# Gate rows as one-column products sent through DRAM, the inverse table moved ahead in the queue, LN2 columns among the first inverse tiles, table scaling on GpSimd

## The chip, the cores and the metric

One core of one Trainium2 chip. The metric is the device time of one execution in microseconds (us). PE is TensorE, DVE is VectorE, ACT is ScalarE, POOL is GpSimd and SP is SyncE, which issues most transfers. PSUM is the memory that PE writes; all other tiles named here lie in SBUF. Timelines are in us from the start of the profiled execution.

## The reference

```python
mod = (silu(c) @ w_mod).reshape(1, 6, 1, 640)
sa, ca, ga, sb, cb, gb = mod[:, 0], ..., mod[:, 5]
h = layernorm(x) * (1 + ca) + sa
x = x + ga * irfft2(rfft2(h) * (w_r + 1j * w_i))          # x: 2048 x 640, bf16
h = layernorm(x) * (1 + cb) + sb
x = x + gb * ((silu(h @ w_gate) * (h @ w_up)) @ w_down)    # 640 -> 1728 -> 640
```

The kernel does the transforms as matmuls with tables. Three stages matter here: the filter (products with the complex filter, in 21 groups of columns), the inverse transform (16 tiles of 128 rows), and the second half, LN2 and the gate and up products. `ga` and `gb` are needed as rows repeated over 128 partitions, `sb` and `cb` (the "LN2 columns") as columns.

## The kernel before

The gate rows come from matmuls whose stationary operand is the gate vector repeated 128 times, so that every partition receives the row:

```python
def mod_bc(j, lo, bank, o=0, ks=range(NC5)):            # 5 matmuls of 320 columns
    gps_ = psum[:, bank, o:o + 320]
    for k in ks:
        nc.tensor.matmul(gps_, lhsT=sc_rep[:, k, :], rhs=wm_r[:, k, j, lo:lo + 320], ...)
```

The queue of SP between the filter's own loads and the weights of the second half:

```python
nc.sync.dma_start(wm_r[:, :, 0, :], wm_m[:, :, 0, :])   # ga weights, before the filter halves
# ... filter halves, tables ...
t2_dma(0); t2_dma(1); t2_dma(2); t2_dma(3)              # transposes of the forward transform
nc.sync.dma_start(wm_r[:, :, 1:3, :], wm_m[:, :, 1:3, :])  # LN2 weights, 1600 KB
nc.sync.dma_start(wm_r[:, :, 3, :], wm_m[:, :, 3, :])      # gb weights, 800 KB
nc.sync.dma_start(Htab[:], H_dram)
nc.sync.dma_start(RI[:], RI_dram)                       # inverse table, 320 KB
```

The seam between filter and inverse transform (the two halves of the table RI are multiplied by `ga` on DVE):

```python
    if g == NG - 1:
        rot(40, 8, slice(0, 64), nc.vector, (1,))       # a rotation: scaled copy, 128 x 512
        nc.vector.tensor_tensor(RI[:, 1], RI[:, 1], ga_bc[:], ALU.mult)
nc.scalar.copy(gb_bc[:, 320:640], mod_bc(3, 320, 3, 128))
s1em(0)                                                 # first inverse tile
s1em(1)
for q0, q1 in ((0, 8), (8, 32), (32, 64)):
    rot(64, 16, slice(q0, q1), nc.vector)
nc.vector.tensor_tensor(RI[:, 0], RI[:, 0], ga_bc[:], ALU.mult)
```

In the inverse loop, at tile 4, the first chunk of LN2 is transposed by DMA (tile `h2T`), and at tile 10 POOL scales it (four of its five parts; ACT the fifth); the first gate product of PE reads it, just before the products of the last tile:

```python
    if t == 4:
        ln2_tr(0)                                       # transpose by DMA: h2T
        load_gu(512, 1024, (1,))
    if t in (10, 13):
        ln2_mod(0, range(4) if t == 10 else range(4, 5))   # scaling on POOL, then the fifth on ACT
    if t == NT - 1:
        fin13 = gu13(0, at_of(0))                       # first gate product
```

## Time and profile before

| | before |
|---|---|
| median of 3 runs | 250.89 us (250.81 to 251.66) |
| span of the profiled run, mean clock | 249.1 us, 0.998 |
| PE busy | 98% |
| first product from a transposed column group starts on PE | 42.60 us |
| last filter product of DVE ends | 60.26 us |
| first inverse product (L1149) | 64.75 us |
| h2T: transpose issued, POOL scales from | 71.83, 77.80 us |
| first gate product, then the run of gate products | 81.28, 82.38 us |

The prediction below shows the lines for most of this. First the chain of work that ended last, as shares of the span by engine:

```profile
PE 80%; SPq 9%; DMA 6%; ACT 1%; DVE 1%; issue 1%; DVEq 0%; ACTq 0%
```

Then, from DVE's timeline (start, duration, line, operation, output<-input), one of the last rotations, 0.28 us for 512 columns, and the multiplication of one half of RI by `ga`:

```profile
62.39 0.28 DVE L646 TENSOR_SCALAR rE<-rE 128x512 bf16<-128x512 bf16 x1
62.59 0.48 DVE L711 TENSOR_TENSOR rH<-rH,ga_bc 128x640 bf16<-128x640 bf16 x1
```

### The profile page before, as it was taken

The page shows a single profiled execution, that of the slowest core. Times are in us where ns is not written, and L with a number is a line of the kernel's source. Part 1 is how long each engine was busy: PE and PEld are TensorE (multiplying, and loading weights), DVE is VectorE, ACT ScalarE, POOL GpSimd, SP SyncE. Part 2 cuts the span into 40 slices and gives each one's busy share as a digit, 9 for nine tenths or more (in the row PEclk, how much of TensorE's full clock was granted, in tenths as well). Part 3 has the DMA queues.
Part 4 walks back from the last instruction along what each step waited for, and adds up shares of the span by engine and source line. Part 5 has one row for each costly group of instructions (what it writes and reads, how often), then busy time and mean ns, then how long its engine had stood idle before and what let it go on. Part 6 is the DMA issues. An engine that isn't in the chain of part 4 may idle for free.

```text
span 249.1 us, 6473 instructions
## 1 busy us (share of the span) xinstructions
PE 243.5 (98%) x2512; PEld 200.4 (80%) x2512; DVE 209.7 (84%) x524; ACT 162.7 (65%) x300; POOL 74.3 (30%) x122
## 2 busy tenths in 40 slices
PE   8999999999999999999999999999999999999994
PEld 3778877999889888688877778886768887779973
DVE  4798888998898997879997997879995888895895
ACT  3778666997788798488862487674356766235740
POOL 8487755894025422000003900001330000440000
PEclk9999999999999999999999999999999999999999
DMA  7999999999999999300005020003311000211001
GB/s 221 396 357 334 309 365 191 175 397 381 286 352 288 275 264 186 81 9 0 3 0 108 13 68 29 3 3 58 73 42 39 3 0 3 54 53 57 3 0 53
DMA packets 45760, 34.43 MB, mean 138 GB/s; under 512 B 21731, under 2 KB 42658, under 8 KB 45346
## 3 DMA queue, kind: packets, MB, share of 16 engines
q1 hardware_dynamic: 43936, 30.00, 42.8%
q0 software_dynamic: 1504, 3.95, 6.7%
q8 instruction: 19, 0.31, 0.5%
q10 hardware_dynamic: 290, 0.08, 0.1%
q14 instruction: 11, 0.09, 0.1%
HBM read 26.72 MB, written 4.72 MB: 126 GB/s over the span
## 4 chain that ended last, share of the span: by engine, by line
PE 80%; SPq 9%; DMA 6%; ACT 1%; DVE 1%; issue 1%; DVEq 0%; ACTq 0%
PE psum L1016 33%; PE psum L899 19%; PE psum L986 9%; DMA rW<-wflip_r 4%; PE psum L879 3%; PE psum L597 3%; PE psum L664 3%; PE psum L567 2%; SPq L273 2%; SPq L277 2%; PE psum L1149 2%; DMA rM<-in_w_mod_dram 2%; SPq L275 2%; PE psum L1152 2%; PE psum L974 2%; PE psum L618 2%
## 5 line engine op out<-in xcount | busy, mean ns | idle before, releaser
L1016 PEld LDWEIGHTS <-rW 128*128 128x128 bf16 (+1 forms) x528 | 46.9, 98 | 5.6 <-issue 0.2
L1016 PE MATMUL psum<-rW 128*128 128x256 bf16 (+1 forms) x240 | 27.1, 259 | 0.0
L913 POOL TENSOR_TENSOR rM<-rM,rL 128x320 f32<-128x320 f32 x6 | 5.9, 975 | 68.2 <-ACT rL L912 68.2
L899 PEld LDWEIGHTS <-rE 128*128 128x128 f16 (+1 forms) x196 | 19.1, 97 | 7.7
L1016 PE MATMUL psum<-rY,rW 128*128 128x256 bf16 (+1 forms) x96 | 24.0, 259 | 0.0
L986 PE MATMUL psum<-rW 128*128 128x256 bf16 (+1 forms) x170 | 23.1, 291 | 0.0
L899 PE MATMUL psum<-rE 128*128 128x320 f16 (+1 forms) x147 | 22.3, 299 | 0.0
L590 DVE TENSOR_TENSOR rM<-psum,rW 128x384 bf16<-128x384 f32 (+2 forms) x42 | 20.1, 541 | 2.0 <-PE psum L567 1.4
L986 PEld LDWEIGHTS <-rW 128*128 128x128 bf16 x170 | 16.6, 98 | 3.8
L1016 PEld LDWEIGHTS <-rE 128*128 128x128 f16 x192 | 17.4, 98 | 2.4
L899 PEld LDWEIGHTS <-rX 128*128 128x128 bf16 (+1 forms) x151 | 14.6, 97 | 5.4
L760 POOL TENSOR_TENSOR rstd<-rstd,mhalf 128x4 f32<-128x4 f32 (+2 forms) x4 | 4.5, 1120 | 48.2 <-DVE rstd L756 48.2
L1052 DVE TENSOR_TENSOR rH<-psum,rW 128x512 bf16<-128x512 f32 x21 | 14.5, 689 | 4.9 <-PE psum L1016 3.1
L1048 ACT COPY rH<-psum 128x512 f32<-128x512 f32 x21 | 12.3, 585 | 9.0 <-PE psum L1016 7.3
L1042 ACT COPY rW<-psum 128x512 f32<-128x512 f32 x21 | 12.3, 585 | 6.8 <-PE psum L1016 6.7
L1055 ACT COPY rX<-psum 128x512 f32<-128x512 f32 x21 | 12.3, 586 | 6.7 <-PE psum L1016 6.7
L1070 DVE TENSOR_TENSOR rX<-rH,rL 128x512 bf16<-128x512 bf16 x21 | 8.9, 423 | 9.1 <-ACT rL L1068 9.0
L382 DVE SCALAR_TENSOR_TENSOR rE<-rE,mv,psum 128x648 bf16<-128x648 f32 (+1 forms) x17 | 14.2, 844 | 2.1 <-PE psum L318 1.5
L1056 DVE TENSOR_TENSOR rX<-psum,rX 128x512 f32<-128x512 f32 x21 | 14.4, 685 | 1.7 <-ACT rX L1055 1.6
L899 PE MATMUL psum<-rA,rX 128*128 128x320 bf16 (+1 forms) x98 | 15.6, 299 | 0.0
L1016 PE MATMUL psum<-rH,rW 128*128 128x256 f16 (+1 forms) x96 | 15.1, 259 | 0.1
L1016 PE MATMUL psum<-rE,rY 128*128 128x256 f16 (+1 forms) x96 | 15.1, 259 | 0.0
(198 smaller groups left out, 674.3 us busy)
## 6 DMA issues: line engine op xcount, KB each, us to landing
out_dram<-rA SPq DMA_DIRECT2D x31, 80.0 KB, 1.6
rM<-in_w_mod_dram SPq DMA_DIRECT2D x3, 800.0 KB, 9.9
rX<-in_A_x_dram SPq DMA_DIRECT2D x3, 640.0 KB, 7.3
rA<-in_B_w_down_dram SPq DMA_DIRECT2D x2, 960.0 KB, 14.4
rM<-in_w_mod_dram SPq DMA_DIRECT2D x1, 1600.0 KB, 7.1
rY<-in_B_w_gate_dram POOLq DMA_DIRECT2D x2, 768.0 KB, 7.7
rW<-in_B_w_gate_dram SPq DMA_DIRECT2D x2, 640.0 KB, 7.2
rW<-in_B_w_up_dram SPq DMA_DIRECT2D x2, 640.0 KB, 6.5
```

The lines of the kernel that those rows point to most:

```text
L382: nc.vector.scalar_tensor_tensor(Zv[:, h], Cv[:, h], mv[:, t, 0:1], zps[:, h], ALU.mult, ALU.subtract)
L590: nc.vector.tensor_tensor(PP[:, :, hl], xv[:, :, hl], in1, ALU.mult)
L597: nc.tensor.matmul(yps[:, i, :], lhsT=_rev(PP, 64 * n * ps + i, [[n, 128]]), rhs=identb[:], start=(ps == 1 and i == 0), stop=(ps == 0 and ...
L899: nc.tensor.matmul(o, lhsT=lhsT, rhs=rhs, start=start, stop=stop, skip_group_check=True)
L986: nc.tensor.matmul(gu[u], lhsT=Wgu[:, u, c5, ff * 128:(ff + 1) * 128], rhs=h2T[:, :, c5, :], start=(c5 == 0), stop=(c5 == NC5 - 1))
L1016: nc.tensor.matmul(o[:, f], lhsT=w, rhs=b, start=(start and f == 0 and i == 0), stop=(stop and f == F - 1 and i == len(ops) - 1), skip_gro ...
L1042: nc.scalar.copy(c0, X)
L1048: nc.scalar.copy(c2, X)
L1052: nc.vector.tensor_tensor(c11, Z, c0, ALU.add)
L1055: nc.scalar.copy(c3, X)
L1056: nc.vector.tensor_tensor(c22, Y, c3, ALU.add)
L1070: nc.vector.tensor_tensor(ato, v4(c11), v4(g21), ALU.mult)
```

## The change

Its intent is to take work off PE and DVE. The 20 matmuls of 320 columns give way to 50 one-column products, which make the gate as five columns; those are transposed by a small matmul, written to DRAM as one row and read back into all 128 partitions. The ga weights move behind the filter halves, so the filter lands earlier; RI moves ahead of the transposes; the LN2 weights go to the end of this stretch of the queue; the LN2 columns are made between the first inverse tiles, instead of in the filter's last groups; and POOL, not DVE, multiplies RI by `ga`. The core of the diff (cuts marked):

```diff
-    nc.sync.dma_start(wm_r[:, :, 0, :], wm_m[:, :, 0, :])
...
         nc.sync.dma_start(Ktab[:, 0:384], K_dram[:, 0:384])
+        nc.sync.dma_start(wm_ga[:], wm_m[:, :, 0, :])
+        nc.sync.dma_start(RI[:], RI_dram)
...
-        t2_dma(3)
-        nc.sync.dma_start(wm_r[:, :, 1:3, :], wm_m[:, :, 1:3, :])
-        nc.sync.dma_start(wm_r[:, :, 3, :], wm_m[:, :, 3, :])
-        nc.sync.dma_start(Htab[:], H_dram)
-        nc.sync.dma_start(RI[:], RI_dram)
+        def g_row(i, eng, row):
+            eng.dma_start(row[:], bass.AP(tensor=g_dram[i].tensor, offset=g_dram[i].offset, ap=[[0, P], [1, D]]))
+        def mod_col(o, w, c5):                       # five one-column products
+            for k in range(NC5):
+                nc.tensor.matmul(o, lhsT=w[:, k, 128 * c5:128 * c5 + 128], rhs=sc_col[:, k:k + 1], ...)
...                                                  # in stage_a
+            if g == 7:
+                nc.sync.dma_start(wm_r[:, :, 2, :], wm_m[:, :, 3, :])      # gb weights
+                g_write(0, nc.sync)
+                t2_dma(3)
+                g_row(0, nc.sync, ga_bc)
+                nc.sync.dma_start(Htab[:], H_dram)
+                nc.sync.dma_start(wm_r[:, :, 0:2, :], wm_m[:, :, 1:3, :])  # LN2 weights
...
+        wsum(Wn, 0, 16, nc.vector)                   # filter sums, cut smaller
...
+            if g == 4:
+                wsum(Wn, 16, 32, nc.vector)
...
+            if g == NG - 5:
+                g_write(1, nc.gpsimd)
+                ri_fold(1)                           # RI[:, 1] times ga, on POOL
...
+                rot(40, 8, slice(0, 64), nc.vector)  # both rotations of the last group, on DVE
-                rot(40, 8, slice(0, 64), nc.vector, (1,))
-                nc.vector.tensor_tensor(RI[:, 1], RI[:, 1], ga_bc[:], ALU.mult)
...
-        nc.scalar.copy(gb_bc[:, 320:640], mod_bc(3, 320, 3, 128))
-        s1em(0)
-        s1em(1)
+        ri_fold(0)
+        for t in range(2):
+            s1em(t)
+            if t == 0:
+                b_cols(0)                            # LN2 columns
+        g_row(1, nc.gpsimd, gb_bc)
...
-        nc.vector.tensor_tensor(RI[:, 0], RI[:, 0], ga_bc[:], ALU.mult)
+        VTs = {0: s1er(0)}
+        b_cols(1)
+        VTs[1] = s1er(1)                             # and tiles are then prepared two ahead
```

## The prediction

> **What bounds the kernel now.** I read the page's busy shares first, then the chain of work that ended last in order of time, then the timelines of the DMA-issuing queue, VectorE (DVE), TensorE (PE) and GpSimd (POOL) around the two seams that the diff touches.
>
> The page says that PE is nearly always busy, so only PE work taken off, or PE idle time closed, can count:
>
> ```profile
> PE 243.5 (98%) x2512; PEld 200.4 (80%) x2512; DVE 209.7 (84%) x524; ACT 162.7 (65%) x300; POOL 74.3 (30%) x122
> ```
>
> The chain in order of time (start us, us, what) has one stretch that is not PE: the first 40 us are the DMA queue, ending in the flipped filter half, then one DVE sum of that filter, then the filter products (L590):
>
> ```profile
> 23.38 3.89 SPq L279
> ...
> 29.07 9.58 DMA rW<-wflip_r
> ...
> 38.74 0.44 DVE rW L407
> ...
> 39.68 1.02 DVE rM L590 x2
> ...
> 40.75 0.49 PE psum L567 x4
> ```
>
> L279 is the load of the gate weights for ga (800 KB); it is queued ahead of the flipped filter that ends the wait. From 42.6 us to the end, the chain is PE almost without a break. DVE's timeline across this seam:
>
> ```profile
> 35.46 0.95 DVE L407 TENSOR_TENSOR rW<-rW 128x1536 bf16<-128x1536 bf16 x1
> 36.89 0.49 DVE L542 TENSOR_TENSOR rM<-psum,gb_bc 128x256 bf16<-128x256 bf16 x2 [0.49 <-ACT rA L400]
> 37.81 0.56 DVE L590 TENSOR_TENSOR rM<-psum,rW 128x384 bf16<-128x384 f32 x1 [0.43 <-PE psum L567]
> 38.74 0.43 DVE L407 TENSOR_TENSOR rW<-rW 128x512 bf16<-128x512 bf16 x1 [0.37 <-DMA rW<-wflip_r]
> 39.21 4.88 DVE L590 TENSOR_TENSOR rM<-psum,rW 128x384 bf16<-128x384 f32 x11
> ```
>
> Eleven products run without a gap, 4.88/11 = 0.444 us each: until about 44 us DVE is the limit. PE waits twice for it, 0.29 us each, at 40.75 and at 42.60:
>
> ```profile
> 42.60 0.41 PE L567 MATMUL psum<-Ktab,rL 128*128 128x192 bf16 x3 [0.29 <-DVE rM L590]
> ```
>
> After that PE is limited by itself, at 1.0 to 1.1 us a group of filter columns. The second seam, from the filter to the inverse transform, has the matmuls that the change removes (L651) and those it moves (L571):
>
> ```profile
> 57.43 0.35 PE psum L571 x15
> ...
> 62.16 0.68 PE psum L651 x5
> 62.84 0.97 PE psum L664 x16
> 63.81 0.22 PE psum L669 x4
> 64.04 0.68 PE psum L651 x5
> 64.75 0.31 PE psum L1149
> ```
>
> A third place matters because a shift has to pass through it: the transposed LN2 tile (h2T), which POOL scales at L786 before the first gate product L974 of PE at 81.28 us:
>
> ```profile
> 77.80 2.50 POOL L786 TENSOR_SCALAR rW<-rW,one_p_cb,modcols 128x256 bf16<-128x256 bf16 x4 [7.12 <-DMA rW<-rL]
> ```
>
> POOL waits 7.12 us for that transpose. It is issued at 71.83 us behind weight loads, and the DMA rates stay above 320 GB/s until about 75 us: its landing is set by the bytes queued ahead of it.
>
> **What the Trainium skill says.** "TensorE: Matmul & The Clock Gate", section "Wait — 56ns, not 53.3ns?", gives N/2.4 GHz + 2.5 ns between warm matmuls and a floor of about 25 ns start to start. The trace agrees: five 320-column matmuls take 0.68 us of the chain, 136 ns each (the formula gives 135.8), and fifteen one-column ones 0.35 us, 23 ns each. So the 163 ns mean of one such record is latency and not cost. "DMA: Bandwidth & Descriptors", section "Queues, rings and completion order", says that each DMA engine consumes one queue's descriptors in ring order; so what is put earlier in the queue delays what follows. The trace agrees as far as it can: the first transposes' data flows only once the loads issued before them have drained, about 38.2 us for an issue at 36.76. The same page, section "Anatomy of one DMA", gives about 2 us fixed per transfer, mostly the receipt; here the 80 KB output stores land 1.6 us after issue. A write to DRAM and a read back should therefore cost some 4 us of latency plus the queue ahead.
>
> **The change part by part.**
>
> (a) Gate rows. Removed: 20 matmuls of 320 columns, 20 x 0.136 = 2.72 us of PE. Ten (ga, 1.36 us) lie at 35.9 to 39.4 us, where PE waits for DVE and DMA anyway: worth nothing of their own. Ten (gb, 2 x 0.68) are on the chain at 62.16 and 64.04: 1.36 us. Added: 50 one-column products, 50 x 0.023 = 1.15 us, and two 128-column transposing matmuls, 2 x 0.056 = 0.11. The 25 for ga fall at about 42 us, where PE has its DVE waits (mostly free); the 25 for gb (0.58) fall on PE's dense stretch.
>
> (b) LN2 columns moved from the last four filter groups to the first two inverse tiles. 50 x 0.023 = 1.15 us leaves one dense PE stretch and enters another: nothing in PE time. But the two DVE idle times that they make (0.36 at 55.5, 0.58 at 58.1) close too, so DVE can follow. (a) and (b) together on the dense PE path: removed 1.36, added 0.58 + 0.11, so 0.67 us gained.
>
> (c) The load of the ga weights goes behind the flipped filter. 800 KB at the 420 GB/s of that stretch is 1.9 us: the filter should land at about 36.7 instead of 38.65. The DVE sum of it is then done before the first products, and the 0.95 us sum of 48 columns is cut into two of 0.42, one of which fits into the 0.43 us wait ahead of 37.81, one goes to group 4, the third to POOL. My DVE count: 35.46 + 0.42 (Wn) to 35.9, wait to 36.7, 0.43 (Wv) to 37.1, 0.49 to 37.6, 0.42 to 38.0, two products to 38.9. Before, the second product ended at 39.65. Gain 0.75 us for DVE.
>
> (d) The inverse table RI (320 KB) now stands ahead of the first transposes: 0.33 MB/420 GB/s = 0.8 us more queue on the late rings, about 0.5 us on the landing, 41.3 to 41.8. With POOL's 0.26 us addition the first group from a transpose starts at 42.1 us on PE, against 42.60: so 0.5 of the 0.75 passes to PE. The copies of the gate columns and rows (4 x 0.15 to 0.2) and the 0.42 us sum in group 4 take up most of the rest of DVE's lead by 46 us. I carry 0.45 us.
>
> (e) Tail. DVE loses the two RI multiplications (2 x 0.48) and two copies of gate and columns; ACT loses 0.47 of gb copy; POOL gains two folds of 640 columns, from its 1.15 us for 512 estimated at 1.45 us each. POOL has idle times of 1.30 at 57.3 and 2.08 at 59.8, and no L786 until 77: it fits. Tile 0 is evacuated in two parts and tiles are prepared two ahead; PE's gaps between inverse tiles add up to 17.08 us for 15 intervals less 15 x 1.11 = 0.4 us, of which I count 0.2.
>
> Sum to the first gate product: 0.45 + 0.67 + 0.2 = 1.3 us. Then the third place: with h2T landing unchanged, POOL ends at 80.3, so PE's 81.28 can come forward by at most about 0.95 us. The loads ahead are the same bytes in another order, less 320 KB sent earlier, plus 160 KB of gate row: about 0.3 us earlier by bytes. Cap 0.95 + 0.3 = 1.2 us, and uncertain by half a microsecond, as the row's round trip holds the queue. I expect 1.0 us: 250.89 - 1.0 = **249.9 us**.
>
> **The rivals.** First: the transposes become the wait. For it: RI and the ga weights stand before them, and their landing had only 1.0 us of POOL idle behind it. Against: the drain is uneven over rings, and early ones lose nothing. It would leave (a) and (b): 250.2 us. Second: the DRAM round trip holds up the queue. The last transpose now waits for the ga row of group 7 (about 45.5 us, against 43.81), and takes 5.4 us to land: 51.5. Its addition on POOL came at 53.24 and would come near 52.5: it just fits. If it misses, PE stands for up to 1 us: 251 us. Third: h2T's landing binds fully or comes later, since the table and LN2 weights are issued about 2 us later: no gain at all, 250.9 us. Fourth, upward: nothing of this binds and the prefetch takes all gaps: 0.75 + 0.67 + 0.4 = 1.8 us, 249.1 us.
>
> **Range and chances.** The fourth gives the low end with a little spare, the third the high end: 248.9 to 250.8 us. Faster by over 2% would need 5 us, and all the PE work removed is 2.7: chance 0.01. Slower by over 2% would need a new stall of 5 us; the second rival would have to miss by far: 0.02. Within 2%: 0.97.
>
> **What would show it.** Right: the chain no longer holds the filter's landing as a 9.6 us piece ending in a DVE wait; the eleven-product run of DVE starts 0.5 to 1 us earlier; no 320-column L651-like matmuls; the first inverse product (L1149 before) starts at 63.3 to 63.8 instead of 64.75; POOL's scaling of h2T starts at 77.3 to 77.8. Wrong: PE or POOL waiting over 0.5 us for a transpose into rL or rM, or PE waiting for POOL's h2T scaling near 80 us; a wait for the inverse table or for the gate row; or a down-stream stage (from 82 us) whose own length changed by more than 0.3 us, which my sum takes as fixed.

## The result, and the profile after

| | before | after |
|---|---|---|
| median | 251.13 us (250.81 to 251.66, 4 runs) | 254.25 us (253.21 to 255.20, 4 runs) |
| profiled span | 249.1 us | 252.2 us |
| transposed group starts on PE | 42.60 | 43.02 |
| the fifth group after that | 47.24 | 48.46 |
| last filter product of DVE ends | 60.26 | 61.05 |
| first inverse tile runs on PE (after: but for one product at 62.71) | 62.84 | 64.28 |
| first inverse product | 64.75 | 66.59 |
| h2T issued, scaled from | 71.83, 77.80 | 74.24, 82.29 |
| first gate product on PE | 81.28 | 82.89 |
| run of gate products | 82.38 | 85.51 |

The kernel became 1.2% slower: ratio 1.0121, 95% interval 1.0075 to 1.0167. A ratio here is the mean time of one kernel's fast runs over that of the other's fast runs of the same rounds, so not quite the ratio of the medians quoted; in the experiments, executions made for a profile are left out of it. From the run of gate products on, the second half takes the same 166.7 us in both profiles, so the loss of 3.1 us is complete when the gate products start, and is to be found before that.

On the page PE has fewer busy microseconds than before and yet a smaller share, for the span grew:

```profile
PE 242.8 (96%) x2544; PEld 200.2 (79%) x2544; DVE 211.9 (84%) x526; ACT 161.9 (64%) x298; POOL 78.0 (31%) x125
```

The chain that ended last, by engine, tells who took PE's place in it: DVE, DMA and POOL, with "issue" for waits that the profile can't name.

```profile
PE 73%; SPq 9%; DMA 8%; DVE 3%; issue 3%; POOL 2%; ACT 1%; DVEq 0%; POOLq 0%; ACTq 0%
```

From 38.4 to 48.4 us the chain goes mostly through ACT, POOL and DVE, with a sum of DVE (L409) in it, and "issue" after it. From there on it has two stretches that are not PE, at the second seam and at h2T:

```profile
62.22 0.26 DVE rE L666
62.48 1.38 issue
63.85 0.29 DVE rE L666
...
64.28 0.55 PE psum L675 x7
...
74.24 7.85 DMA rW<-rL
...
82.29 2.41 POOL rW L816 x4
```

Two rotations of DVE (L666) with 1.38 us between them, for which nothing that the profile knows is responsible, hold the first inverse tile. The transpose of h2T with POOL's scaling holds the gate products. The list of PE's waits (for what, us in total, how often, longest) names the same two:

```profile
PE psum L675 <- DVE rE L666: 1.4, 1, 1.4
PE psum L1004 <- POOL rW L816: 1.0, 3, 0.5
```

DVE's timeline answers to the lines in the prediction. The first sum waits for the filter only until 36.94, and the run of products starts at 38.20, as foretold. But a sum of 512 columns, 0.42 us at its first appearance, takes 1.21 us at 44.21, and the two rotations 1.92 us together, where before one took 0.28:

```profile
36.94 0.42 DVE L409 TENSOR_TENSOR rW<-rW 128x512 bf16<-128x512 bf16 x1 [1.17 <-DMA rW<-wflip_r]
...
38.20 4.58 DVE L610 TENSOR_TENSOR rM<-psum,rW 128x384 bf16<-128x384 f32 x10
...
44.21 1.21 DVE L409 TENSOR_TENSOR rW<-rW 128x512 bf16<-128x512 bf16 x1
...
62.22 1.92 DVE L666 TENSOR_SCALAR rE<-rE 128x512 bf16<-128x512 bf16 x2
```

POOL's timeline shows what ran beside them:

```profile
42.88 2.26 POOL L409 TENSOR_TENSOR rW<-rW 128x512 bf16<-128x512 bf16 x2
...
62.36 1.41 POOL L694 TENSOR_TENSOR rH<-rH,ga_bc 128x640 bf16<-128x640 bf16 x1
```

POOL's fold of RI (L694) runs from 62.36 to 63.77, and DVE's second rotation starts at 63.85. POOL's two sums end at 45.14, and DVE's stretched sum is over just after.

A third difference is in the transfers. In windows of 4 us (the last column is GB/s, the one before it the busy share of the DMA engines), the kernel before moves 404 GB/s from 52 to 56 us and the kernel after half of it:

```profile
52.00:56.00 4.00, 4.00 (x80) 4.00 (x78) 3.59 (x9) 3.98 (x7) 3.74 (x7) 1.00 1.08 404
```

```profile
52.00:56.00 4.00, 4.00 (x79) 3.80 (x77) 3.43 (x9) 3.36 (x6) 3.97 (x7) 1.00 0.68 207
```

That is where the row of `ga`, issued at 51.20 us, is read into 128 partitions: from the issue, 160 KB take 4.6 us to land, with the weights behind it.

### The profile page after: what moved, and what is told of

It is laid out like the page before. It is cut to its first block, busy times and chain, and to the rows that moved or that the text cites.

```text
span 252.2 us, 6550 instructions
## 1 busy us (share of the span) xinstructions
PE 242.8 (96%) x2544; PEld 200.2 (79%) x2544; DVE 211.9 (84%) x526; ACT 161.9 (64%) x298; POOL 78.0 (31%) x125
## 4 chain that ended last, share of the span: by engine, by line
PE 73%; SPq 9%; DMA 8%; DVE 3%; issue 3%; POOL 2%; ACT 1%; DVEq 0%; POOLq 0%; ACTq 0%
PE psum L1046 32%; PE psum L929 19%; PE psum L1016 9%; DMA rW<-wflip_r 3%; DMA rW<-rL 3%; PE psum L909 3%; SPq L276 2%; SPq L280 2%; PE psum L617 2%; PE psum L579 2%; SPq L282 2%; DMA rM<-in_w_mod_dram 2%; SPq L278 2%; PE psum L1004 2%; PE psum L675 1%
## 5 line engine op out<-in xcount | busy, mean ns | idle before, releaser
L1182 DVE SCALAR_TENSOR_TENSOR rM<-psum,rX 128x640 f32<-128x640 f32 x16 | 13.1, 820 | 3.3 <-PE psum L1180 3.2
```

The source lines that it names most:

```text
L1182: nc.vector.scalar_tensor_tensor(x1[:, t, :].rearrange("p (m r) -> p m r", r=4), ops.rearrange("p r m -> p m r"), 1.0, x_sb[:, t, :].rearr ...
```

## The experiments

Eighteen kernels ran, all with correct results, each timed against the kernel before in the same rounds, on four different chips, so kernels are compared by their ratios. They ask four questions: is DVE stretched because POOL works beside it; is the read of one row slow; does RI's new place delay the transposes; and why does h2T land so long after its issue. A note on the expectations: no variant of the changed kernel had a median under 252.92 us, so an expectation among the first twelve of a time clearly below that was missed, even where its mechanism showed. In the diffs, "-" lines are those of the kernel named.

### DVE beside POOL

**The first fold back on DVE** (kernel after):

```diff
-        ri_fold(0)
         for t in range(2):
             s1em(t)
...
+        nc.vector.tensor_tensor(RI[:, 0], RI[:, 0], ga_bc[:].rearrange("p (m r) -> p r m", r=4), ALU.mult)
         VTs = {0: s1er(0)}
```

> Changed kernel, with the second half of the inverse table scaled by ga on VectorE (after its rotations) instead of on GpSimd. Theory of the shared port: VectorE's two rotations took 1.92 us instead of 0.56 because GpSimd's 1.41 us scaling ran beside them; without it the two rotations take under 0.7 us and the first inverse tile (64.28) starts near 63.0. By the queue theory the time gains less than the 1.3, because the transposed LN2 tile still lands near 81 to 82: 252.8 to 254. If the rotations stay near 1.9 us with no GpSimd work beside them, the port theory falls.

Measured: 253.23 us, ratio 1.0034 (0.9995 to 1.0073). DVE's two rotations:

```profile
61.30 0.54 DVE L666 TENSOR_SCALAR rE<-rE 128x512 bf16<-128x512 bf16 x2
```

So 0.54 us instead of 1.92. In the 16 profiles of the changed kernel and its variants the two take 1.90 to 2.56 us in all eight that fold on POOL at this place, and 0.53 to 0.94 in all eight that don't. The first inverse tile starts at 61.8 instead of 64.28, but then PE waits 1.0 us for the LN2 weights, the last load in the queue, and runs at half clock for 3.4 us from 64.3 on.

**POOL's fold in the kernel before**, as a control:

```diff
             if g == NG - 1:
+                nc.gpsimd.tensor_tensor(RI[:, 0], RI[:, 0], ga_bc[:], ALU.mult)
                 rot(40, 8, slice(0, 64), nc.vector, (1,))
...
-        nc.vector.tensor_tensor(RI[:, 0], RI[:, 0], ga_bc[:], ALU.mult)
```

> The kernel before, with one of the two scalings of the inverse table on GpSimd beside VectorE's rotations. Port theory: VectorE's next operation with two SBUF inputs or its next rotation starts 1.1 to 1.4 us late behind the GpSimd scaling, the first inverse product moves from 64.75 to 65.6 or later, and the time rises by 0.6 to 1.2 us. Rival (VectorE has 0.48 us less to do, engines don't meet): unchanged or 0.2 faster, rotations at 0.28 us each.

Measured: 252.63 us, ratio 1.0059 (1.0031 to 1.0086). DVE loses an instruction of half a microsecond and the kernel gets slower. The instruction of DVE that now stands beside the fold, its other multiplication of the table, takes 1.68 us, for 0.48 in the kernel before; POOL's fold ran from 64.05 for 1.49 us:

```profile
64.20 1.68 DVE L712 TENSOR_TENSOR rH<-rH,ga_bc 128x640 bf16<-128x640 bf16 x1
```

The blocking follows the fold into the other kernel. (In this profile the first transpose also came late, its addition at 42.50 us instead of 41.34, so the profile's later times are not used. From DVE's last filter product to the first inverse product it takes 5.32 us, 4.49 in the kernel before.)

**The DVE sum of group 4 joined to the early one** (kernel after), out of the way of POOL's sums:

```diff
-        wsum(Wn, 0, 16, nc.vector)
+        wsum(Wn, 0, 32, nc.vector)
...
-            if g == 4:
-                wsum(Wn, 16, 32, nc.vector)
```

> Changed kernel, with the filter sum of columns 16 to 32 joined to the one of 0 to 16 on VectorE before the first products, where GpSimd has nothing to do. Port theory: the sum in group 4 took 1.21 us because GpSimd's sums ran until 45.14; joined it costs some 0.25 us more, in a stretch where VectorE later waits 0.62 for a transpose anyway. Group 8 starts at 45.7 instead of 46.41 and later groups 0.6 to 0.8 earlier. Rival (the loss in these groups comes from the transposes alone): no shift after group 5. Time: 0 to 0.8 us less than the changed kernel, as the LN2 tile caps it.

Measured: 254.21 us, ratio 1.0089 (1.0049 to 1.0129). The joined sum takes 0.68 us for both parts, against 0.42 and 1.21, and the filter runs 0.7 to 1.0 us earlier (its group at 59.35 comes at 58.47). Of that, 0.39 us is there at the first transposed group already, before the sum could matter. From this group to the fifth after it, it takes 4.80 us instead of 5.44: 0.64 us is what the sum's new place gives. At the end little of it is left: PE still waits for h2T and the gate products start at 85.08, not 85.51.

### The read of one row, and the order of the queue

**Gate rows in 16 copies** (kernel after): the row is written 16 times, and each copy is read by 8 partitions, instead of one row by 128:

```diff
-            eng.dma_start(row[:], bass.AP(..., ap=[[0, P], [1, D]]))
+            eng.dma_start(row[:], bass.AP(..., ap=[[D, 16], [0, 8], [1, D]]))
```

> The changed kernel, with each gate row written to DRAM as 16 copies, read by 8 partitions each, instead of one row read by all 128. In the changed kernel the DMA queue moves 207 GB/s at 52 to 56 us, against 404 before, and is 0.8 MB (2 us) behind for the rest. Theory: 128 reads of the same 1280 bytes are slow (about 120 GB/s while they run), so with 16 copies that stretch comes to 260 GB/s or more, the transposed LN2 tile lands 0.5 to 1 us earlier, time 0.3 to 1 us less than the changed kernel (ratio to before 1.008 to 1.011). Rival: the hole is the latency between the last transpose and the table load, which waits behind the gate row in issue order; then nothing changes.

Measured: 253.32 us, ratio 1.0036 (0.9998 to 1.0074). The window that moved 207 GB/s:

```profile
52.00:56.00 4.00, 4.00 (x73) 3.80 (x71) 3.54 (x9) 3.10 (x7) 4.00 (x7) 1.00 0.94 311
```

Nothing else changed in the queue: 128 reads of the same 1280 bytes are what is slow. From the first of the row's 128 packets until nine tenths of them have started it takes 1.9 to 2.4 us in the eleven profiles that read one row by SP, and 0.7 to 1.1 in the four with copies. The landing does not show it: 4.69 us after the issue, for 4.61. By 60 us 18.51 MB have been moved, against 17.99 in the kernel after and 18.63 before; but in the two later kernels with copies whose first transposes were not disturbed (all repairs, without and with 56 matmuls) about 18.1, no more than without copies. What the copies are worth in bytes for the rest of the queue, and so in time, is shown by this one profile alone. h2T is issued at 73.41 and the gate products start at 84.24.

**The loads at once, the row on POOL's queue** (kernel after): gb weights, last transpose, Htab and LN2 weights issued straight after the third transpose, and the row of `ga` written and read through POOL's queue.

```diff
         t2_dma(2)
+        nc.sync.dma_start(wm_r[:, :, 2, :], wm_m[:, :, 3, :])
+        t2_dma(3)
+        nc.sync.dma_start(Htab[:], H_dram)
+        nc.sync.dma_start(wm_r[:, :, 0:2, :], wm_m[:, :, 1:3, :])
...
-            if g == 7:  (the same loads, g_write and g_row on SP)
+            if g == 7:
+                g_write(0, nc.gpsimd)
+            if g == 10:
+                g_row(0, nc.gpsimd, ga_bc)
```

> Changed kernel, with the last transpose, the inverse table and the LN2 weights issued right behind the first three transposes without waiting for the ga row; the ga row's write and read go through GpSimd's own queue. Queue theory: the queue runs full some 3 us sooner, the transposed LN2 tile lands at 79 to 80.5 instead of 82.29, and PE's wait of 2 us before the gate products goes: 1.2 to 2 us less than the changed kernel (252.2 to 253.0). Rival (the LN2 tile is late only because its inputs are late): it still lands about 8 us after issue and the time stays at 254.

Measured: 255.84 us, ratio 1.0143 (1.0106 to 1.0180), a miss. The slow read moved to 57 to 59 us and landed 6.9 us after its issue; the rates were 305 and 299 GB/s in the two windows from 52 to 60; POOL was later, and its fold blocked DVE's rotations for 2.56 us. Moving the row to another queue does not help.

**RI behind the first transposes** (kernel after):

```diff
-        nc.sync.dma_start(RI[:], RI_dram)       # ahead of the transposes
...
         t2_dma(2)
+        nc.sync.dma_start(RI[:], RI_dram)
```

> Changed kernel, with the inverse table RI (320 KB) issued behind the first three transposes instead of before them. Theory: RI's bytes ahead of the first transpose delay its landing from 41.34 to 42.66; behind them it lands at 41.6 to 42.0 and group 5 starts near 42.3 instead of 43.02. Rival: the ga weights ahead are what delays it (then no change). Time 0 to 0.7 us less than the changed kernel; less of it if VectorE's 1.21 us sum then binds.

Measured: 254.51 us, ratio 1.0098 (1.0057 to 1.0139). POOL's addition to the first transposed tile starts at 41.58 us instead of 42.70, and the group at 42.11 instead of 43.02. That RI's place does it is not shown. Over the twelve profiles with RI ahead and no fetch moved into the first transpose, the addition starts between 41.78 and 42.70, on average at 42.17; with RI late at 41.58 here and at 42.05 in the other such run (all of these repairs together, below); in the kernel before and two variants of it, without RI there, at 41.34, 41.79 and 42.50. So the 42.70 of the kernel after is the late end of what its queue gives, and RI is worth about 0.3 us in these means, less than single profiles differ.

### Other places for the LN2 columns

**LN2 columns at the fourth inverse tile** (with the first fold on DVE):

```diff
             s1em(t)
-            if t == 0:
-                b_cols(0)
...
-        b_cols(1)
         VTs[1] = s1er(1)
...                                     # in the inverse loop
+            if t == 3:
+                b_cols(0)
+                b_cols(1)
```

> The run with RI's second half scaled on VectorE, and besides the LN2 columns moved from the first two inverse tiles to the fourth (they are needed only at the tenth). In that run PE idled about 1.2 us at 62.3 to 63.5 for the LN2 weights and its clock then fell to half for some 3.5 us. Queue theory: without these columns there PE goes through from the filter to the inverse, the first inverse product starts near 63.7 instead of 65.96, the clock stays at 1.0, and what is left is the wait for the transposed LN2 tile: the time is 0.5 to 1.2 us under the run before it (252.0 to 252.7 against 252.0 of the kernel before on that chip). If PE still idles there over 0.5 us, another input was behind the LN2 weights (the inverse table).

Measured: 253.93 us, ratio 1.0113. The first inverse product is early (64.48), but DVE's fold holds up the second half of the products of that tile by 0.6 us, and the columns cost almost 2 us at tile 3. h2T is issued at 74.45.

**All of these repairs together** (the last one, the joined sum, RI late):

> The four repairs that do not touch the last transpose: RI scaled on VectorE, LN2 columns at the fourth tile, the filter sum joined early, RI behind the first transposes. If my sum for the start was right but for these, group 5 starts near 42.1, group 8 near 45.0, the first inverse product near 62.7 to 63.3 (before: 64.75). The time is then set by the transposed LN2 tile: if that stays near 81 to 82, 251.5 to 252.5, no better than the kernel before; if it follows, 250 to 251.

Measured: 254.95 us, ratio 1.0119. RI late pushes the last transpose and the weights back: POOL waits 2.1 us for the former and PE's weight load 0.6 for the latter (those of gb), and h2T is scaled from 83.35. Its edit is the sum of the three shown.

**Fold on DVE after the first small rotation, both column sets behind the second tile, joined sum** (kernel after):

```diff
-        ri_fold(0)
         for t in range(2):
             s1em(t)
-            if t == 0:
-                b_cols(0)
...
             if q0 == 0:
-                nc.vector.tensor_copy(modcols[:, 2, :], psum[:, 3, 192:197])
+                nc.vector.tensor_tensor(RI[:, 0], RI[:, 0], ga_bc[:].rearrange("p (m r) -> p r m", r=4), ALU.mult)
         VTs = {0: s1er(0)}
-        b_cols(1)
         VTs[1] = s1er(1)
+        b_cols(0)
+        b_cols(1)
+        nc.vector.tensor_copy(modcols[:, 2, :], psum[:, 3, 192:197])
```

> The changed kernel, with the tail mended without new waits: RI's second half scaled on VectorE right after the first rotation, both sets of LN2 columns behind the two inverse tiles (not in front of the first), the filter sum joined early. The run with these columns at the fourth tile gained 2.1 us at the first inverse product but lost 1.8 us at the fourth tile. Theory: first inverse product near 64.0 to 64.8, PE clock 1.0, no halved tiles; the transposed LN2 tile is issued about 1 us earlier than 74.24 but lands when the queue lets it (80.5 to 82), so PE still waits 1 to 2.5 us before the gate products: ratio to before 1.002 to 1.008. If it falls under 1.002, the queue was not the limit.

Measured: 253.43 us, ratio 1.0065 (1.0023 to 1.0107). The first inverse product comes at 65.25 instead of 66.59 (64.0 to 64.8 was expected), and h2T is issued at 72.90; but it is scaled only from 81.72, 8.8 us after its issue.

### Why h2T lands late

**A late gate load**: 640 KB of gate weights go behind the transpose instead of ahead of it, in three kernels.

```diff
-    load_gu(512, 1024, (0,))
...
-                load_gu(512, 1024, (1,))
+                load_gu(512, 1024)
```

In the kernel after:

> The changed kernel, with one of the gate weight loads (640 KB) issued behind the transposed LN2 tile instead of ahead of it. Queue theory: the tile lands 1.5 to 2 us after 80.5 less, near 80 instead of 82.3, PE's wait before the gate products goes down by 1.5 us or ends; 252.3 to 253.2 against 254.25. Rival (the landing is late because the transpose itself is slow or issued late): still about 8 us from issue to landing, time unchanged.

With the previous experiment's edits:

> The run above, and besides the 640 KB of gate weights issued behind the transposed LN2 tile. Queue theory: the tile lands 6 to 6.5 us after its issue, near 79.5, PE does not wait for it; the time is 1 to 2 us under the run above, at or just under the kernel before (ratio 0.995 to 1.001). Rival (the tile is late because its own transpose is slow): same time as the run above.

In the kernel before, as a control:

> The kernel before, with the same 640 KB issued behind the transposed LN2 tile: the control. PE did not wait for that tile there (0.3 us of slack), so nothing to gain: ratio 0.997 to 1.003. If it is faster by over 0.5%, the queue was already a limit before the change and I misread the kernel before.

Measured: 253.83 us, ratio 1.0092 (1.0057 to 1.0127); 252.92 us, 1.0037 (1.0002 to 1.0073); 251.69 us, 0.9992 (0.9945 to 1.0038). From issue to scaling, h2T takes 5.7, 7.8 and 4.3 us. In the control the load ahead is worth 1.7 us of landing and nothing of the time, because POOL had room there. But in the second, with that load out of the way too, the transpose still took 7.8 us: the bytes ahead of it do not explain that. This left the question open.

Read finely, the transfer shows what happens. h2T arrives as 1280 packets of 256 bytes. The view of the transfers in the kernel after, from 78.4 to 81.6 us; the row is the GB/s in 40 equal parts, 0.08 us each, and the second line is the queue by which instructions are fetched:

```profile
GB/s 10 90 19 102 22 74 61 90 35 70 93 291 477 266 278 272 266 221 16 6 0 0 0 0 0 6 6 10 6 10 10 10 10 10 13 150 341 384 410 384
...
q8 instruction: 1, 0.02, 2.1%
```

The packets flow at some 270 GB/s, then there is a stretch of 1.3 us with at most 16 GB/s, and then the rest comes. One packet of the instruction queue is in the window: by the packet records it lasted from 79.36 to 80.45 us, and h2T's packets stop entirely from 79.94 to 80.44. The kernel after has 20 such packets of 16 KB (before: 19), each taking 0.9 to 1.4 us, and PE has 5088 matmuls and weight loads, about 254 for each packet, so they are PE's. "Runtime: NRT & Kernel Launch", section "Instruction fetch mechanics", says the same: instructions come in blocks of 16 KiB, 256 of them, by a DMA queue. The same stretch in the kernel before lies at 45.3 to 46.5 us, behind a fetch at 44.8, in the third of the first transposes, where nothing waits for it (44 to 47 us):

```profile
GB/s 205 222 215 222 218 215 222 215 249 195 447 191 218 150 89 31 20 0 0 0 0 0 3 7 10 7 10 10 10 7 10 10 14 246 283 290 264 270 297 294
```

The theory is then: a fetch of PE's instructions that falls into a DMA transpose leaves one engine behind with its share, and the transpose waits about 1.3 us for it. (That one engine is held is inferred, here as below.) In the kernel before the fetch comes at 80 us, when h2T is long there; in the kernel after h2T is 2.4 us later, and the fetch at 79.3 hits it. Its rival: a backlog of other loads, for which the fetch is a bystander. The fetch can be moved without touching the transfers, by matmuls that do nothing.

**63 more matmuls at the start**: nine matmuls of 512 columns that PE does on ones in its idle time of the first 30 us are cut into 72 of 64. In the kernel after:

```diff
-    def idle_pe(n, w=4):
-        for i in range(n):
+    def idle_pe(n, w=4, cut=False):
+        for i in range(8 * n if cut else 0):
+            nc.tensor.matmul(banks(5, 1, [64]), lhsT=ones[:], rhs=ones[:, 0:64], start=True, stop=True)
+        for i in range(0 if cut else n):
             nc.tensor.matmul(banks(5, 1, [128 * w]), ...)
```

> The kernel after, with the nine 512-column idle-time matmuls of the first 30 us cut into 72 of 64 columns: 63 more matmuls and weight loads (126 instructions) in PE's stream, about 30 ns each in place of 0.21 us, so no PE time. Theory (fetch): PE's instructions come in packets of 16 KB (20 in the kernel after, one for each 128 or so matmuls with their loads), each holding one DMA engine 0.9 to 1.4 us; the one at 79.2 us lies inside the transpose of the LN2 tile, and the pieces of it on that engine trickle in from 80.4 to 81.2 us after all others have landed at 79.8. Moved 63 matmuls forward it falls at 74 to 76 us, before the transpose's data; no trickle is left, and GpSimd's scaling starts at 80.6 to 81.0 us instead of 82.29. PE then waits less: gate products start at 84.0 to 84.4 instead of 85.5, median 253.0 to 253.4. Rival (the backlog of loads alone makes the transpose late, the trickle is whatever engine drains last): the trickle stays, and scaling starts at 82 us or later, 254.2.

In the kernel before:

> The kernel before with the same 63 extra matmuls. Its fetch at 80.0 us should move to about 75.3 us, into the transpose of the LN2 tile (data from 74.2 to 77.0). Theory (fetch): the trickle of about 35 packets a us on one engine now appears here too, GpSimd's scaling starts at 78.8 to 79.3 instead of 77.8, its end at 81.3 to 81.8 against PE's arrival at 81.28, so PE waits 0 to 0.5 us and the median is 250.9 to 251.5 against 251. Rival: no trickle, scaling at 77.8, same time.

Measured: 255.48 us, ratio 1.0170 (1.0141 to 1.0198), and 252.88 us, ratio 1.0063 (1.0044 to 1.0082). In the first, the fetch came at 75.9 us, the slow stretch was gone from h2T (first to last packet 2.0 us, for 4.4), scaling began 4.8 us after the issue, for 8.05, and PE waited for nothing there. But both kernels lost elsewhere: another fetch moved from 44 to 41 us, into the first transpose, and PE waited 1.3 us for it in both. In the kernel before, between 41 and 43.4 us:

```profile
GB/s 282 550 265 282 265 277 265 282 260 73 0 0 0 0 0 0 0 0 9 9 4 13 9 9 9 13 4 13 9 13 9 9 48 269 286 282 294 299 286 282
```

and what PE made of it:

```profile
44.01 0.42 PE L569 MATMUL psum<-Ktab,rL 128*128 128x192 bf16 x3 [1.32 <-POOL rL L561]
```

So 63 matmuls that cost PE nothing make the kernel before 0.63% slower; its profile has 1.3 us of that as PE's wait behind a fetch. The fetch theory missed in one point: in the kernel before, h2T showed the slow stretch too, as expected, but was scaled 5.5 us after its issue, no later than without (6.0).

**All repairs that had shown a gain**, without and with those 63 matmuls: the last tail, the late gate load and the 16 copies.

> All repairs that showed a gain, on the kernel after: joined early sum of Wn, the first table fold on VectorE after the first rotation piece, LN2 columns behind the second inverse tile, the late gate load behind the transpose, and the gate rows written as 16 copies. Without the shift of instructions. The two halves (0.37 and 0.36 per cent above before) repair different things (VectorE behind GpSimd; the slow row read): transposes and weights come as in the run with 16 copies, rotations in 0.54 us. Expected: h2T issued at 72.4 to 72.7, scaling at about 80 us because of the fetch at 77 to 78 us, PE waits about 0.8 us, median 251.8 to 252.4 against 251.4 for before. If the slow row read costs nothing of its own: as the run without copies, 252.3.

> The same with the 63 extra idle-time matmuls, so that the fetch falls before the transpose. Theory (fetch): no trickle, scaling starts at 78.2 to 79.0, PE does not wait for it beyond 0.3 us, gate products start at 81.6 to 82.3, median 250.2 to 251.2: level with before or up to 0.4 per cent under it. Rival: as the run without the shift.

Measured: 253.61 us, ratio 1.0087 (1.0065 to 1.0108), and 253.64 us, ratio 1.0090 (1.0064 to 1.0116). Both missed. Without the shift h2T was issued at 72.91 and, with a fetch at 78.9, scaled 8.8 us later; PE waited 1.8 us. With it, h2T took 4.35 us, but the first transpose was hit (addition at 44.13, PE waiting 1.1 us).

**56 one-column matmuls ahead of the first inverse tile**, so that only the later fetches move. In the kernel after, where PE waits there anyway, and in the repaired kernel:

```diff
+        for i in range(56):
+            nc.tensor.matmul(psum[:, 3, 448:449], lhsT=ones[:], rhs=ones[:, 0:1], start=True, stop=True)
         for t in range(2):
             s1em(t)
```

> The kernel after, with 56 one-column matmuls ahead of the first inverse tile, where PE waits 1.35 us for the blocked rotations anyway: at 24 ns each they fit into that wait, and every fetch of PE's instructions after them comes 56 matmuls earlier, those before them stay. (In the two shifted runs, the shift from the start of the kernel moved the fetch at 44 us to 41 to 42 us, into the first transpose, whose addition then started at 43.4 to 44.1 us; that is avoided here.) Theory (fetch): the first transpose as in the kernel after (addition at about 42.7), the fetch that lay at 79.2 comes at 75 to 76, the transpose of the LN2 tile lands about 5 us after its issue instead of 8.05, so scaling starts at about 79.5 and PE (at 82.9 to 83.2) waits for nothing; gate products start at 84.0 to 84.4 instead of 85.51; median 252.7 to 253.2. Rival (the transpose was faster in the shifted runs only because it was issued 2 us later, behind a drained queue): landing still 7 to 8 us after issue, and 254.2 or more.

> All repairs of the run of that name, with the same 56 one-column matmuls; here PE waits only about 0.2 us at that place, so they cost about 1.1 us of PE. Theory: the transpose issued at about 73.5 to 74 lands 5 to 6 us later, scaling starts at 79 to 79.8, PE comes at about 82.3 and waits at most 0.3 us; gate products at 83.4 to 83.9 instead of 85.0 in the run without; median 252.2 to 252.9 against 253.6. Rival: no gain on the run without them, 253.6 or more.

Measured: 254.31 us, ratio 1.0100 (1.0068 to 1.0132), and 253.42 us, ratio 1.0053 (1.0011 to 1.0094); both medians missed. The profiles show what was expected in kind. In the first, the fetch came at 75.8, the slow stretch behind it was gone, and scaling started 6.3 us after the issue, for 8.05 (about 5 was expected). From 77.4 to 80.6 us, in parts of 0.08 us:

```profile
GB/s 346 422 387 167 374 253 304 330 304 234 205 138 61 131 77 38 115 42 26 70 77 38 70 32 16 16 19 19 154 298 291 282 298 291 282 298 328 387 374 371
```

What is left is a slow stretch in the middle of h2T, before its main flow, of which more below. PE waited for nothing, and the gate products started at 84.57 instead of 85.51. In the second, scaling started 5.1 us after the issue instead of 8.8, and the gate products at 83.29 instead of 85.01, although PE had 1.3 us more to do. The medians tell less: the first did not become faster than the kernel after (its profiled run, 253.22, was the fastest of six, the others up to 255.38), the second is 0.2 us below its sister, which the intervals do not separate; its six runs go from 251.92 to 254.88. So the mechanism is shown in the profiled executions; a gain in time from repairing it is not. One candidate for the reason stands in the windows of the first (64 to 66 and 66 to 68 us; the third column from the end is PE's granted clock):

```profile
64.00:66.00 2.00, 2.00 (x49) 2.00 (x47) 1.30 (x8) 0.65 (x2) 0.65 (x1) 0.64 1.07 363
66.00:68.00 2.00, 2.00 (x33) 1.77 (x31) 0.12 (x1) 0.89 (x2) 0.00 (x0) 0.50 1.23 249
```

PE ran at half clock for some 3.4 us, in and after the stretch of one-column products. One such dip takes the mean clock of the whole execution to about 0.993. A mean clock of 0.993 or less is in 36 of 75 executions of the changed kernel and its variants (in four of the six of this one, two of the four of the kernel after), and in none of 43 of the kernel before and of 14 of its variants. Within a kernel, executions with it are 0.57 us slower on average (standard error 0.22). Not every dip is of this place: of nine profiles that have one, in seven it starts at 64 to 67 us, and in two (the tail, and the first run of all repairs together) at 84.2 and 85.7, where PE had just waited for h2T. "TensorE: Matmul & The Clock Gate", section "What's actually happening", has a free-running window of 3413 ns of little activity as the cause of half clock, which fits both the length and that only some executions of a kernel have it.

### All runs of h2T side by side

Times from the packet records of each profile: the fetch nearest to h2T, first and last packet of h2T, and the issue to the start of scaling. "In" means that the fetch lies between first and last packet. "Slow" is the longest stretch, in us, in which all transfers together ran below 20 GB/s between the first packet and the scaling, read in parts of 0.05 us. (In parts of 0.1 us single packets weigh less: then the kernel before has 0.4 and the kernel after with 56 matmuls 0.3, and the other profiles without a fetch at most 0.1.)

| kernel | ratio of times | issue | packets | fetch | slow | issue to scaling | gate products from |
|---|---|---|---|---|---|---|---|
| before | 1 | 71.83 | 74.0–77.0 | 80.1 | 0.15 | 5.97 | 82.38 |
| before, late gate load | 0.9992 | 72.43 | 74.3–75.9 | 80.1 | 0 | 4.25 | 82.98 |
| before, fold on POOL | 1.0059 | 74.27 | 76.6–78.9 | 72.4, 82.5 | 0.05 | 5.30 | 84.83 |
| before, 63 matmuls | 1.0063 | 73.83 | 76.1–78.7 | 76.3, in | 1.1 | 5.53 | 84.38 |
| after | 1.0121 | 74.24 | 76.8–81.3 | 79.3, in | 1.3 | 8.05 | 85.51 |
| fold on DVE | 1.0034 | 74.48 | 76.7–81.1 | 77.4, in | 1.4 | 7.39 | 85.12 |
| joined sum | 1.0089 | 73.36 | 76.5–81.0 | 77.4, in | 1.25 | 8.45 | 85.08 |
| loads at once | 1.0143 | 77.45 | 79.3–82.2 | 79.8, in | 1.2 | 5.50 | 87.36 |
| RI late | 1.0098 | 74.42 | 77.1–80.8 | 79.3, in | 0.95 | 7.49 | 85.13 |
| LN2 columns late | 1.0113 | 74.45 | 76.5–79.6 | 79.4, in | 0.1 | 7.49 | 84.92 |
| those together | 1.0119 | 74.24 | 78.4–82.4 | 80.6, in | 1.1 | 9.11 | 87.23 |
| late gate load | 1.0092 | 75.46 | 77.5–80.3 | 78.0, in | 1.3 | 5.71 | 85.11 |
| 16 copies | 1.0036 | 73.41 | 75.8–80.0 | 76.7, in | 1.35 | 7.63 | 84.24 |
| tail | 1.0065 | 72.90 | 77.0–80.9 | 78.2, in | 0.05 | 8.82 | 85.68 |
| tail, late gate load | 1.0037 | 72.72 | 75.0–79.6 | 77.9, in | 1.2 | 7.84 | 83.89 |
| all repairs | 1.0087 | 72.91 | 75.6–80.5 | 78.9, in | 1 | 8.78 | 85.01 |
| after, 63 matmuls | 1.0170 | 76.55 | 78.5–80.5 | 75.9 | 0.05 | 4.77 | 86.35 |
| all repairs, 63 matmuls | 1.0090 | 76.27 | 78.4–79.9 | 73.8 | 0 | 4.35 | 85.92 |
| after, 56 matmuls | 1.0100 | 74.92 | 77.6–80.4 | 75.8 | 0.05 | 6.33 | 84.57 |
| all repairs, 56 matmuls | 1.0053 | 73.64 | 75.6–77.8 | 73.3 | 0 | 5.08 | 83.29 |

Of the 13 profiles with a fetch in h2T, 11 have a slow stretch of 0.95 to 1.4 us; of the seven without, none has more than 0.15. In each of the eleven h2T's packets stop for 0.3 to 0.6 us, and the next one starts 0.01 to 0.02 us before the fetch ends. That speaks against the rival, a backlog of other loads, as a backlog need not end with the fetch. In one of the two exceptions (LN2 columns late) the fetch came with the last packets, and the scaling started 2.2 us after them, where 0.7 to 1.2 is usual. From first to last packet h2T takes 2.7 to 4.9 us, 3.9 on average, with a fetch in it, and 1.5 to 3.0, 2.2 on average, without. That the two ranges overlap says that a fetch is not the only thing that stretches it. There is a second slow stretch, in the middle of h2T: from a quarter to half of its packets it takes 1.2 us in the kernel before, 1.5 in the kernel after and 1.7 in that with 56 matmuls, with no fetch there, but 0.3 in the kernel before with the late gate load. Both kernels have it, so it is not what sets them apart; no run asks for its cause.

## Why the prediction was wrong

The expected sign was wrong and the value outside the range. Here its own sum is set against the two profiles, in differences to the kernel before (us, minus is earlier). Its 0.67 us of (a) and (b) are split by stretch: LN2 columns out and gb columns in, 1.15 − 0.58 − 0.11 = 0.46 earlier in the filter; gb rows out and LN2 columns in, 1.36 − 1.15 = 0.21 among the first tiles. The second seam is the time from the last filter product of DVE to PE's next work, 60.26 to 62.16 before and 61.05 to 64.28 after.

| step of the prediction | expected | measured |
|---|---|---|
| filter lands (c) | 36.7 us | 36.85 us |
| start of the dense filter stretch (c, d) | −0.45 | +1.22 |
| dense filter stretch: LN2 columns out, gb columns in (a, b) | −0.46 | −0.43 |
| DVE at the second seam (e) | fits | +1.33, PE waits |
| first tiles: gb rows out, LN2 columns in (a, b) | −0.21 | −0.28 |
| inverse stage: two tiles ahead (e) | −0.2 | −0.23 |
| PE at the first gate product | −1.3 | +1.61 |
| h2T: scaling from | 77.3 to 77.8 us | 82.29 us |
| gate products | −1.0 | +3.13 |

**What held.** Everything that was counted in PE's own instructions: one-column products at 23 to 24 ns each, their move between the stretches, the removed matmuls, the tiles prepared ahead. These terms sum to −0.87 expected and −0.94 measured. The filter's landing held too, and DVE's products did start 1.0 us earlier.

**What failed first: durations of DVE taken from a row in which POOL was not beside it** (steps c, d and e). The prediction used 0.42 us for the sum in group 4 and found that POOL's folds "fit" into POOL's idle times; it asked whether POOL had room, not what DVE does meanwhile. The sum took 1.21 us, 0.79 more, and the rotations 1.38 more, of which PE waited 1.33 to 1.35. "SBUF — State Buffer", section "Who interferes with whom", which the prediction did not consult, says that DVE and POOL share a pair of ports as an exclusive lock for a whole instruction, that copies and `tensor_scalar` on DVE can take it, and that two SBUF inputs contend with a POOL instruction that reads SBUF. The traces agree: 0.54 against 1.92 us with and without the fold on DVE, and 0.48 against 1.68 when the fold was brought into the kernel before. That page also says that an instruction with at most one SBUF input, outside its 2-port modes, does not contend; DVE's products from PSUM indeed kept their pace (4.58 us for ten, 0.458 each, against 0.444 before).

**Not shown to have failed: RI ahead of the transposes** (step d). It was put at 0.5 us, and PE's first transposed group at 42.1. In the profile of the kernel after POOL's addition came 1.36 us later than before and this group 0.42 later. But in eleven other profiles with RI ahead the group came at 42.09 to 42.71, and the addition varies as much without RI as with it. So the 0.42 in the start's +1.22 may be luck of one profile. The other 0.80 lies between this group and the fifth after it (5.44 us, for 4.64 before); 0.64 of it is gone where the stretched sum is (4.80 in five of the seven profiles with the joined sum, 5.2 in two).

**Failed in its principle: h2T "set by the bytes queued ahead"** (the cap of step e). Fewer bytes ahead and 0.3 us earlier was the estimate; it was 4.5 us later. First, the issue came 2.41 us later, since it waits for inverse tiles, which were late. The prediction treated it as fixed. Second, the landing took 2.08 us longer. The spread from first to last packet grew by 1.5 us, with a stretch of 1.3 us behind an instruction fetch; when the fetch was moved away this stretch was gone in each of the four profiles. The rest is put down to the queue, which is argued, not shown: the read of one row by 128 partitions cost about half the transfer rate for 4 us (207 GB/s for 404; 311 with 16 copies). The third rival of the prediction named this outcome ("comes later: no gain at all") but took 250.9 us for its worst case; a landing past PE's arrival costs more than the gain.

**Not needed for the loss**: the second rival. The last transpose was issued at 47.95 us, later than the 45.5 supposed, but landed after 4.5 us and did not make PE wait. (The prediction's sum there is off: 45.5 and 5.4 give 50.9, not 51.5. And its stated range ended at 250.8, below the 250.9 and 251 of two of its own rivals. The section that it cites for 2 us a transfer is about transfers issued by GpSimd; the row of `ga` went by SP.)

**What stays open.** Single repairs bring the ratio from 1.0121 to 1.0034 (fold on DVE) or 1.0036 (16 copies), and all of them together to 1.0087 or, with 56 idle matmuls, 1.0053. No variant of the changed kernel has a ratio below 1, though the intervals of those two single repairs reach down to it; and only these two and the tail with the late gate load have an interval that lies below that of the kernel after. The gains do not seem to add, and why is shown only in part: each repair moves the issue of h2T and the fetch against each other, and executions with a dip of PE's clock, about half of them, are 0.6 us longer. One profile a kernel cannot tell how often each happens in the executions that were only timed. How much of the median's 3.1 us is the fetch is therefore not settled; in the profiled execution it is at most the 1.5 us (3.13 less 1.61) by which PE waited for h2T's scaling.

## What to carry to other kernels

Before moving an operation to GpSimd because it has idle time, look at what VectorE does in the same microsecond: here scaled copies and operations on two SBUF tiles stood until the GpSimd instruction ended, 0.8 to 1.4 us, and the profile showed it only as a longer duration or as "issue". A wait that had about one microsecond of room (here POOL's scaling of the transposed tile, done at 80.30 for 81.28) belongs into the sum with everything that sets its issue, as a shift upstream is added to it in full. And a DMA transpose near the critical path should have slack of more than a microsecond, for in 11 of 13 profiles it stood for about 1.3 us where an instruction fetch fell into it, and 56 or 63 more matmuls of PE moved the fetches by 3 to 6 us.

## What the Trainium skill lacked or had wrong

- "Runtime: NRT & Kernel Launch", section "Instruction fetch mechanics", calls the cost of a 16 KiB boundary mostly hidden. It was hidden from PE, but not from a DMA transpose in flight: in 11 of 13 profiles with a fetch in h2T all transfers ran below 20 GB/s for 0.95 to 1.4 us (for some 280 before), in none of the seven others; and 63 idle matmuls that shifted a fetch into the first transpose made the kernel before 0.63% slower. That the fetch holds one DMA engine, and so its share of the transpose, is inferred; the trace does not name the engines.
- "TensorE: Matmul & The Clock Gate" explains half clock by idle windows. Here PE was busy without a gap, with 56 one-column products, 8 of a tile and 25 more of one column, when the clock fell for 3.4 us (mean clock 0.64 and 0.50 from 64 to 68 us); 36 of 75 executions of the changed kernel and its variants, which have 25 or more such products in a row, show a dip, none of 57 of the kernel before and its variants, which have at most 15. Other dips follow waits of PE of 1 to 2 us in all. The page does not say how little work on the array counts as idle.
- No page that we found has the cost of reading one DRAM row into 128 partitions: nine tenths of the packets took 1.9 to 2.4 us to start, with 16 copies of the row 0.7 to 1.1; the rate of all transfers over 4 us fell to 207 GB/s, with the copies to 311 (in one profile).
- No page that we found says how much the arrival of a DMA transpose varies: the 320 KB of h2T, 1280 packets of 256 bytes, took from 1.5 to 4.9 us from first to last packet.
